# Reordering a hand-scheduled kernel of two state-space layers: 26 moves in the list of operations, five of them with another engine or form

## The chip, the cores and the metric

The kernel runs on one core of one Trainium2 chip. Its time is the device time of that core for one execution, in microseconds (us); of several executions the median is taken. The core has five engines with queues of their own, each in order: TensorE (PE, with its weight loads shown as PEld), VectorE (DVE), ScalarE (ACT), GpSimd (POOL) and SyncE (SP), which issues nearly all DMAs. Matrix products land in PSUM, eight banks of 128 x 512 float32, and are copied from there ("evicted") by DVE or ACT.

## The reference

Two independent layers on sequences of 2048 steps and 640 channels, their results side by side in bf16. Layer A is a diagonal complex recurrence, layer B a gated long convolution.

```python
# A
Lam_bar = exp(dt * Lam); B_bar = ((Lam_bar - 1) / Lam)[:, None] * Bmat
Bu = einsum("bld,pd->blp", x, B_bar)
h[t] = Lam_bar * h[t-1] + Bu[t]
a = 2 * einsum("blp,dp->bld", h, Cmat).real + x * Dskip
# B
k_shift = sum over 4 taps of shift_k * shifted k
kv = k_shift * v
y = irfft(rfft(kv padded) * rfft(ssm_k padded))[:2048] + kv * ssm_D
b = q * y
out = concatenate([a, b], -1)
```

## The kernel before, in words

The program is a list of 815 small operations, built first and then emitted in an order written out by hand. Every operation has a number, the engines that may run it, what it reads and writes, and, where it uses PSUM, a group that holds one or two banks. The string `ORDER` lists all of them: `266V6` means operation 266, on DVE, bank 6. The letters are A (ACT), V (DVE), G (POOL), T (PE) and S (SP); a small `t` is PE in the narrow form, in which a product with 128 columns of weights is issued as two with 64. The order of one engine's entries is that engine's program order. Between engines only data and banks matter: an instruction waits for the operations whose data it needs, and the first of a group for the last of the group that held its bank.

```python
order = [(int(x[:-2]), x[-2].upper(), int(x[-1])) for x in ORDER.split()]
...
if o is o.group.ops[0]:
    need |= {held[b] for b in own if held[b] is not None}
```

Some entries issue nothing. A product with an addition or multiplication after the eviction (`ev_C`, `er1`) does both at once on DVE; on ACT it only copies, and a following `em_C` or `em1` does the rest. Where the first ran on DVE, the second is empty.

Layer A. The 16 steps of a chunk are treated as a tree: `up2`, `up1`, `up0` (lines 581 and 602, evicted at 598, 622, 648) combine pairs of steps by the tables `rr` (line 457; operations 143 to 146, one for each power), the 128 chunk ends go through a coarse scan, and `dn3` to `dn0` (line 225 or 229, added on DVE at 728 or evicted by ACT at 726) go back down. The coarse scan is done twice, for five blocks each: `cs_v` turns the vector on PE, `cs_v_m` (line 679) multiplies it by a sine, `cs_a` (682) by a cosine, `cs_w` (683) takes the difference, `cs_s` (684) is the scan, then `cs_k`, `cs_k_m` (679), `cs_b` (687) and `cs_h` (690) turn back. The operations of the first are 318 to 326, of the second 327 to 335. `gm` (175, line 457) scales C for `gC` (line 571, evicted at 575); six small copies `cf` (137 to 142, lines 206 and 449) feed it. Last, 16 projections `C0` to `C15` (line 225 wide, 229 narrow) add x times D: `ld_r` (line 736) loads the rows of x, `xd` (737) multiplies them by D's row, which `ld_Dr` (operation 91, line 372) has spread over all partitions, `ev_C` (754) adds, `st_A` (765) stores. `ld_C1` (270 and 272, line 556) loads the last block of C, its real and imaginary half.

Layer B. For each of five blocks of channels, k and v are loaded transposed (`ld_k`, `ld_v`, line 814), four taps are multiplied (`cm`, lines 205 on DVE and 206 on ACT) and added (`ca`, 840), multiplied by v (`cx`, 841), stored to a buffer in DRAM (`pl`, 847) and read back in another layout by eight transfers for each half of the channels (`rl`, 857). The taps of all blocks share one buffer, so block d+1's k is loaded when block d's taps are done. The convolution is a two-stage transform on PE: `s1` (lines 876 wide, 881 narrow, evicted at 886), `s2` (900, evicted at 913), a product on DVE or POOL (`pp`, `pq`, `py`, `pz`, lines 924 to 931), and back by `r2` (951, evicted at 956) and `r1` (972, evicted at 988 or 990). It is run for the filter (`h`, loaded at line 807, and its first row added to at 809) and for kv (`k`), in two halves 0 and 1. The filter of half 1 is loaded into the room of the coarse scan's buffers, so its loads wait for `cs_h1`.

The tables of sines start as integer products on POOL (`wqh` line 309, `gqh` line 350, `cph` line 475, with the counters `w_m`, `g_m`) and become sines on ACT (`w_s` 314, `g_s` 354).

Of the kernel before, what the change touches and what calls it, by code (L numbers as in the profile page):

```python
# [1097 lines left out]
def plain_order(P):  # L1098
# [16 lines left out]


ORDER = (
# [40 lines left out]
)  # L1158


# [68 lines left out]
```

## Time and profile before

| | |
|---|---|
| median of 3 runs | 188.11 us |
| lowest, highest | 187.65, 189.12 us |
| the profiled execution | 187.3 us from its first to its last instruction |
| busy: PE, PEld | 175.6, 126.3 us |
| busy: DVE, ACT, POOL | 158.0, 147.7, 72.6 us |
| granted TensorE clock | 0.999 |
| bytes moved by DMA | 30.15 MB |

The profile is of one execution. Its page gives the span from first to last instruction and no time around it, so the span is taken as that execution's own time. Times of rows are microseconds from the start of the span. A row of the timeline has start, length, engine, line, operation, what it writes and reads, how many instructions, and in brackets how long the engine was idle before and who released it. Operations that are given by number are found in such rows by counting along their engine's order.

### The profile page before, as it was taken

How to read it: one execution, taken by the hardware profiler on the slowest of the kernel's cores; microseconds unless marked ns; L12 is line 12 of the kernel's file. 1: busy time of each engine (PE TensorE's matmuls, PEld its weight loads, DVE VectorE, ACT ScalarE, POOL GpSimd, SP SyncE). 2: the span in 40 equal slices, each digit the busy share in tenths (PEclk: the TensorE clock that was granted, in tenths of full speed). 3: DMA queues.
4: the chain of work that ended last, by engine and by line, in shares of the span. 5: the costliest groups of instructions: out<-in, count | busy, mean ns of one | idle time of the engine just before them, and what ended most of it. 6: DMA issues, size and time to landing. Idle time of an engine off the chain costs nothing.

```text
span 187.3 us, 7665 instructions
## 1 busy us (share of the span) xinstructions
PE 175.6 (94%) x3398; PEld 126.3 (67%) x3399; DVE 158.0 (84%) x225; ACT 147.7 (79%) x181; POOL 72.6 (39%) x68
## 2 busy tenths in 40 slices
PE   7998999999799979979997999999999999999992
PEld 2565666677468756656685688776588876887770
DVE  3537964679959899999969999899999999998961
ACT  2469699989899979999997997997898883985000
POOL 8679999900000000008803925730740000551620
PEclk9999999999999999999999999999999999999999
DMA  5999999799999989999989479402496993058996
GB/s 153 191 184 158 200 143 140 141 174 182 198 253 154 290 179 152 180 182 154 138 109 251 154 170 133 75 5 72 122 196 120 210 227 85 15 160 187 208 219 173
DMA packets 106682, 30.15 MB, mean 161 GB/s; under 512 B 101274, under 2 KB 106010, under 8 KB 106650
## 3 DMA queue, kind: packets, MB, share of 16 engines
q1 hardware_dynamic: 106332, 29.35, 86.7%
q8 instruction: 26, 0.43, 1.1%
q10 hardware_dynamic: 318, 0.33, 0.6%
q14 instruction: 6, 0.05, 0.1%
HBM read 11.32 MB, written 7.86 MB: 102 GB/s over the span
## 4 chain that ended last, share of the span: by engine, by line
PE 54%; DVE 23%; DMA 9%; ACT 8%; issue 3%; DVEq 0%; ACTq 0%
PE acc L225 17%; PE acc L581 13%; DMA arena<-in_B_k_dram 9%; PE acc L229 6%; DVE arena L728 6%; PE acc L900 6%; DVE arena L205 5%; ACT arena L913 5%; PE acc L951 4%; DVE arena L840 3%; PE acc L972 3%; PE acc L539 2%; DVE arena L754 2%; PE acc L881 1%; ACT arena L886 1%
## 5 line engine op out<-in xcount | busy, mean ns | idle before, releaser
L581 PE MATMUL acc<-arena 128*64 128x512 bf16 x400 | 45.6, 380 | 1.8 <-DVE arena L457 1.1
L913 ACT CAST arena<-acc 128x960 bf16<-128x960 f32 (+1 forms) x43 | 37.4, 916 | 4.0 <-PE acc L900 2.2
L225 PE MATMUL acc<-arena 128*128 128x320 bf16 (+2 forms) x255 | 36.4, 297 | 2.2 <-DVE arena L754 1.1
L581 PEld LDWEIGHTS <-arena 128*64 128x64 bf16 x400 | 26.0, 110 | 17.8 <-DVE arena L457 1.3
L886 ACT CAST arena<-acc 128x1024 bf16<-128x1024 f32 x37 | 35.8, 1034 | 2.1 <-PE acc L881 2.0
L225 PEld LDWEIGHTS <-arena 128*128 128x128 bf16 x256 | 23.7, 98 | 12.1 <-DVE arena L754 1.3
L841 POOL TENSOR_TENSOR arena<-arena 128x2048 bf16<-128x2048 bf16 x2 | 8.8, 4410 | 53.7 <-DVE arena L840 46.1
L900 PE MATMUL acc<-arena 128*64 128x160 bf16 x512 | 23.6, 235 | 1.8 <-DVE arena L679 1.4
L900 PEld LDWEIGHTS <-arena 128*64 128x64 bf16 x512 | 18.6, 110 | 8.3 <-ACT arena L913 2.2
L229 PE MATMUL acc<-arena 128*64 128x320 bf16 (+3 forms) x258 | 23.2, 313 | 0.5 <-DVE arena L690 0.5
L840 DVE TENSOR_TENSOR arena<-arena 128x2048 bf16<-128x2048 bf16 x14 | 17.6, 1256 | 4.5 <-ACT arena L206 4.3
L728 DVE TENSOR_TENSOR arena<-acc,arena 128x1024 bf16<-128x1024 f32 (+2 forms) x19 | 20.4, 1114 | 0.9 <-PE acc L229 0.5
L760 POOL TENSOR_TENSOR arena<-arena 128x640 bf16<-128x640 f32 x3 | 4.2, 1416 | 32.6 <-ACT arena L752 32.6
L956 ACT CAST arena<-acc 128x1024 bf16<-128x1024 f32 x16 | 15.4, 1025 | 1.7 <-PE acc L951 1.6
L229 PEld LDWEIGHTS <-arena 128*64 128x64 bf16 x258 | 13.0, 110 | 3.5 <-DVE arena L690 0.6
L876 PE MATMUL acc<-arena 128*64 128x128 bf16 x400 | 14.6, 220 | 0.2 <-ACT arena L886 0.2
L876 PEld LDWEIGHTS <-arena 128*64 128x64 bf16 x400 | 12.9, 110 | 2.4 <-ACT arena L886 0.9
L205 DVE TENSOR_SCALAR arena<-arena 128x2048 bf16<-128x2048 bf16 x15 | 11.0, 749 | 3.6 <-DMA arena<-in_B_k_dram 3.5
L754 DVE TENSOR_TENSOR arena<-acc,arena 128x640 bf16<-128x640 f32 x13 | 10.7, 820 | 3.5 <-PE acc L225 2.2
L206 ACT ACTIVATE arena<-arena 128x2048 bf16<-128x2048 bf16 (+2 forms) x10 | 11.1, 1112 | 1.5 <-DMA arena<-in_B_k_dram 1.5
L924 DVE TENSOR_TENSOR arena<-arena 128x2560 bf16<-128x2560 bf16 x8 | 11.9, 1484 | 0.1
L602 PE MATMUL acc<-arena 128*64 128x256 bf16 (+2 forms) x140 | 11.6, 291 | 0.1
(142 smaller groups left out, 284.4 us busy)
## 6 DMA issues: line engine op xcount, KB each, us to landing
out_dram<-arena SPq DMA_DIRECT2D x32, 160.0 KB, 3.3
arena<-in_B_ssm_k_dram SPq DMA_DIRECT2D x8, 320.0 KB, 6.1
kv_rows<-arena SPq DMA_DIRECT2D x5, 512.0 KB, 4.7
arena<-kv_rows SPq DMA_DIRECT2D x16, 160.0 KB, 4.0
arena<-in_A_x_dram SPq DMA_DIRECT2D x16, 160.0 KB, 3.5
arena<-in_B_q_dram SPq DMA_DIRECT2D x8, 320.0 KB, 6.3
arena<-in_A_B_im_dram ACTq DMA_DIRECT2D x1, 160.0 KB, 2.8
arena<-in_A_B_re_dram SPq DMA_DIRECT2D x1, 160.0 KB, 3.0
```

The source lines that it names most:

```text
L205: vm = lambda e: lambda out, in_, by: e.tensor_scalar_mul(out=out, in0=in_, scalar1=by)
L225: e.matmul(out, lhsT=lhsT, rhs=rhs, start=start, stop=stop, skip_group_check=True)
L229: e.matmul(out[half], lhsT=lhsT[:, half], rhs=rhs, start=start, stop=stop, skip_group_check=True, tile_position=(0, 64 * r))
L581: e.matmul(o[64 * r:64 * r + 64], lhsT=self.BT[j][:, r, d, :], rhs=self.XP[:, d, 2 * q:2 * q + 2], start=(d == 0), stop=(d == 4), skip_gro ...
L728: e.tensor_tensor(out=o, in0=b, in1=o, op=ALU.add)
L754: e.tensor_tensor(out=two(ys), in0=two(B)[:, :, 0:320], in1=two(ys), op=ALU.add)
L840: P.add(f"ca{d}_{j}", tt, lambda e: e.tensor_tensor(out=t1, in0=t1, in1=t2, op=ALU.add), outs=[t1], ins=[t1, t2])
L876: e.matmul(B[64 * b:64 * b + 64, 128 * i:128 * i + 128], lhsT=lh[i], rhs=F[:, b, :], start=True, stop=True, tile_position=(0, 64 * b))
L886: P.add(f"e1{what}{hf}_{u}", {PACT: act(1024), PDVE: dve(1024)}, lambda e, B: c.CP[e](out=out, in_=(B.rearrange("p (l n s k) -> p k s l n" ...
L900: e.matmul(B[64 * s:64 * s + 64, 512 * b + 160 * i:512 * b + 160 * i + 160], lhsT=c.W[:, k, 64 * b:64 * b + 64], rhs=self.AS[hf][:, k, 160 ...
L913: c.CP[e](out=out, in_=b.rearrange("p r (k j n) -> p r k j n", k=n, j=4) if nj > 1 else b.rearrange("p r (k x) -> p r k x", k=n))
L956: P.add(f"er2{hf}_{u}", {PACT: act(1024), PDVE: dve(1024)}, lambda e, B: c.CP[e](out=out, in_=B.rearrange("p (s n b) -> p b s n", s=2, n=4 ...
```

## The change

Only `ORDER` changes. Every operation keeps its bank. On each queue the order differs as follows (names and numbers as in the list; "passes" means that it now comes before):

- SP: D's row `ld_Dr` (91) passes `ld_v3` (445), `ld_r0`, `ld_k4` (455), one half of `ld_C1` (270), `ld_r1` and the four `ld_h1` (439 to 442). `rl0_10` (412) passes five transfers and comes right behind `pl2` (410). `ld_C1` (272) falls behind `rl0_21`, `rl0_31`, `ld_Dr`, `ld_v3`, `ld_k4` and 270. `ld_r0` (724) and `ld_r1` (729) fall behind the four `ld_h1`. The two `ld_B2` (173, 174) change places.
- DVE: the coarse scan's links 319, 321 and 322 come before the taps 447 and 446 of block 3; 325 comes among the additions of block 3, 324 before the tap 451. The table products `rr1` (144) and `gm` (175, with the copy 137 before it) come before `cx0` (387) and `cx1` (398). 133 passes one eviction, 134 falls behind 384 and 385. 679 passes 559, and 715 passes 719.
- ACT: `ev_up20_4` (214) and `w_s` (49) fall behind `ev_up1_2` (238); the copies 142 and 139 come before `e1h0_2` (194).
- POOL: four of the table operations (47, 52, 54, 77) come later; 713 passes 706.
- PE: `cs_v0` (318) passes `s2h0_30` (313); `s2h0_27` (311) falls behind 299 and 259, which change places.
- Another engine or form: `cm0_0` (385) ACT to DVE; `ev_up0b_8` (266) DVE to ACT; `xd2` (735) POOL to DVE; `e2k1_27` (666) ACT to DVE; `dn2_5` (344) from the narrow form to the wide one.

The diff, cut to these places:

```diff
-  ... 173S0 ... 174S0 ... 155S0
+  ... 174S0 173S0 ... 155S0
...
-  ... 380A0 ... 214A2 ... 218A0 ... 49A0 ... 385A0 ... 53A0 ... 75A0 ... 238A0
+  ... 380A0 ... 218A0 ... 384V0 385V0 134V0 ... 53A0 ... 75A0 ... 238A0 214A2 ... 49A0
...
-  ... 387V0 ... 396V0 144V0 ... 135V0 145V0 ... 397V0 ... 398V0 ... 403V0 194A2 137V0 ... 142A0 ... 139A0 ... 175V0
+  ... 144V0 387V0 ... 396V0 ... 135V0 145V0 ... 397V0 ... 138A0 ... 142A0 137V0 139A0 175V0 398V0 ... 194A2 ... 403V0
...
-  320V0 316V0 ... 447V0 301T4 ... 313T0 446V0 ... 318t2 ... 319V2 ... 448V0 ... 321V0 ... 449V0 ... 322V0 ... 450V0 ... 451V0
+  320V0 318t2 319V2 321V0 316V0 322V0 ... 313T0 ... 447V0 ... 446V0 ... 325V0 448V0 ... 449V0 ... 450V0 ... 324V4 451V0
...
-  ... 410S0 415S0 158S0 414S0 416S0 413S0 412S0 272S0 417S0 418S0 445S0 724S0 455S0 270S0 729S0 440S0 441S0 442S0 439S0 91S0 734S0
+  ... 410S0 412S0 415S0 158S0 414S0 416S0 413S0 417S0 418S0 91S0 445S0 455S0 270S0 272S0 440S0 441S0 442S0 439S0 724S0 729S0 734S0
...
-  309T4 ... 311T2 ... 259T6 299T0 ... 266V6 ... 344t4 ... 735G0 ... 666A6
+  309T4 ... 299T0 259T6 311T2 ... 266A6 ... 344T4 ... 735V0 ... 666V6
```

(Each line shows the entries of the queues concerned in their order; "..." are entries left out.)

78 rows, old and new, of the table ORDER are left out of this document.

## The prediction

> **What bounds the kernel now.** I read the page first, then the stretches, then the idle time before each matmul and each VectorE (DVE) operation in order of time.
>
> ```profile
> span 187.3 us, 7665 instructions
> PE 175.6 (94%) x3398; PEld 126.3 (67%) x3399; DVE 158.0 (84%) x225; ACT 147.7 (79%) x181; POOL 72.6 (39%) x68
> ```
>
> ```profile
> 65.20:97.80 32.60, 29.37 (x695) 21.06 (x696) 30.98 (x39) 31.08 (x40) 8.14 (x2) 1.00 1.05 159
> 99.40:183.60 84.20, 83.22 (x1928) 63.74 (x1928) 78.20 (x87) 61.04 (x70) 30.42 (x15) 1.00 0.69 147
> ```
>
> The columns are stretch, length, then busy time of PE, PEld, DVE, ACT and POOL, granted clock (1.00 throughout), DMA share. Two regimes: from 65 to 98 DVE (30.98 of 32.60) and ScalarE (ACT, 31.08) are full while PE idles 3.2 us; from 99.4 on PE is full (83.22 of 84.20). So work saved before 99.4 counts only if the first matmul after 99.37 starts earlier, and what is added after it counts only if PE is made to wait. The three longest waits of PE after 20 us:
>
> ```profile
> 48.12 2.13 PE L581 MATMUL acc<-arena 128*64 128x512 bf16 x18 [1.15 <-DVE arena L457]
> ...
> 67.41 0.61 PE L900 MATMUL acc<-arena 128*64 128x160 bf16 x12 [1.39 <-DVE arena L679]
> ...
> 99.37 2.89 PE L225 MATMUL acc<-arena 128*128 128x320 bf16 x20 [0.97 <-DVE arena L754]
> ```
>
> They are up0a_2 (239) waiting for the table rr1 (144), s2h0_27 (311) waiting for the bank that cs_v0_m (319) drains, and C1 (731) waiting for ev_C0 (727). Together 3.51 us; the change touches the cause of all three.
>
> **The change part by part.** *The table product 144.*
>
> ```profile
> 37.89 1.23 DVE L841 TENSOR_TENSOR arena<-arena 128x2048 bf16<-128x2048 bf16 x1 [1.83 <-DMA arena<-in_B_v_dram]
> ...
> 46.58 1.48 DVE L457 TENSOR_TENSOR arena<-arena 128x1280 bf16<-128x1280 bf16 x1
> ```
>
> It goes from 46.58 to ahead of cx0 (387), where DVE idles 1.83 for the landing of v: 1.48 fits. PE then starts up0a_2 at 46.97 (the end of the matmuls before it), 1.15 earlier. Next late is ACT, which evicts for PE there:
>
> ```profile
> 51.79 1.01 ACT L886 CAST arena<-acc 128x1024 bf16<-128x1024 f32 x1 [0.85 <-PE acc L881]
> 52.82 0.21 ACT L206 ACTIVATE arena<-arena 64x5 bf16<-64x5 f32 x1
> ...
> 58.80 0.22 ACT L206 ACTIVATE arena<-arena 64x5 bf16<-64x5 f32 x1
> ```
>
> The copies 142 and 139 (0.21, 0.22) move into that 0.85 of idle, so e1h0_2 starts near 51.3, not 51.79, and everything behind loses another 0.43: about 0.5 + 0.4 = 0.9 at 60. PE waits for ACT's ev_up0a_4 before up0b_4 (58.67 now), so of the 1.15 some 0.9 arrive at cs_v0.
>
> POOL runs until 37.89 beside the new place:
>
> ```profile
> 35.64 1.25 POOL L475 TENSOR_TENSOR arena<-arena 128x640 int32<-128x640 int32 x1
> 36.85 1.03 POOL L350 TENSOR_TENSOR arena<-arena 128x512 int32<-128x512 int32 x1
> ```
>
> ```profile
> 18.66 3.74 DVE L457 TENSOR_TENSOR arena<-arena 128x1280 bf16<-128x1280 bf16 x2
> ```
>
> Two such products beside POOL took 3.74, so the one that was stretched 2.3 (3.74 less 1.48, and the overlap of 0.08 back). At 2.3, 144 ends at 38.4, cx0 0.5 later, and e1h0_6 (202) behind it at 40.8; up1_0 needs its bank at 41.08: still nothing. The Trainium skill, "SBUF — State Buffer", § SBUF: two separate sides, says that a VectorE operation with two SBUF inputs and a GpSimd one that reads SBUF exclude each other, and the later one blocks fully. The rows show a stretch at most; the sum by it is rival D.
>
> *The product gm (175) and the coarse scan.*
>
> ```profile
> 64.40 0.44 PE L229 MATMUL acc<-arena 128*64 128x512 bf16 x4
> ```
>
> ```profile
> 62.64 1.48 DVE L457 TENSOR_TENSOR arena<-arena 128x1280 bf16<-128x1280 bf16 x1
> 64.05 0.48 DVE L682 TENSOR_TENSOR arena<-arena 128x640 bf16<-128x640 bf16 x1
> ...
> 65.20 1.42 DVE L205 TENSOR_SCALAR arena<-arena 128x2048 bf16<-128x2048 bf16 x2 [0.65 <-DMA arena<-in_B_k_dram]
> 66.53 0.82 DVE L679 TENSOR_TENSOR arena<-acc,arena 128x640 bf16<-128x640 f32 x1
> ...
> 72.10 0.75 DVE L205 TENSOR_SCALAR arena<-arena 128x2048 bf16<-128x2048 bf16 x1
> 72.77 0.82 DVE L679 TENSOR_TENSOR arena<-acc,arena 128x640 bf16<-128x640 f32 x1
> 73.60 0.45 DVE L648 CAST arena<-acc 128x256 bf16<-128x256 f32 x1
> 73.94 0.48 DVE L687 TENSOR_TENSOR arena<-arena 128x640 bf16<-128x640 bf16 x1
> ...
> 78.24 1.49 DVE L684 TENSOR_TENSOR_SCAN arena<-arena 128x640 bf16<-128x640 f32 x1
> ```
>
> gm goes to about 51.3 to 52.8, behind the copies that feed it, ahead of cx1 (398), which becomes about 2 us later; behind cx1 stands the next idle for k2, and its only reader, the store pl1, issues at 58.30: covered. Without gm, cs_a0 (320) starts at 62.65. Now 319 follows at once and waits for PE: cs_v0 ran to 64.84; it is 0.9 earlier and passes s2h0_30 (313), some 0.2 more, so 319 starts at about 63.75 where DVE is free from 63.1: a new wait of 0.65 in place of the old 0.65 for k3. From 62.64 to the end of the second scan (79.73) the sum is: gm 1.41 out (64.05 − 62.64), ev_up0b_8 (266, to ACT) 0.34 out (73.94 − 73.60), the idle 0.65 out, the wait 0.65 in, and 0.35 in for three more pairs in which an operation needs the one just before it (such a pair starts 0.03 after the end, others 0.08 before it). Net −1.4. PE's 1.39 at 67.41 goes, but its next banks wait for ACT, and cs_k1 waits for the second scan: PE, too, gets 1.4. ACT keeps up: it idled 1.0 before ev_up0c_6 here, more than the 0.45 that 266 adds. Conv 3 (447, 446) starts at 66.5, 1.3 later, and ends its taps near 72.9 as before, so ld_k4 is not held up. All of DVE, ACT and PE is then 1.4 earlier up to 95.
>
> *D's row and the transfers.*
>
> ```profile
> 67.63 3.23 SPq L857 DMA_DIRECT2D arena<-kv_rows  x4
> 70.90 1.79 SPq L556 DMA_TRANSPOSE arena<-in_A_C_im_dram  x1
> ...
> 82.93 7.61 SPq L807 DMA_DIRECT2D arena<-in_B_ssm_k_dram  x4
> 90.58 3.45 SPq L372 DMA_DIRECT2D arena<-in_A_Dskip_dram  x1
> ```
>
> ```profile
> 95.96 0.53 DVE L809 TENSOR_TENSOR arena<-arena 128x80 bf16<-128x80 bf16 x1
> 97.87 0.49 DVE L737 TENSOR_TENSOR arena<-arena 128x640 bf16<-128x640 bf16 x1 [1.38 <-DMA arena<-in_A_Dskip_dram]
> ```
>
> ld_Dr (91) leaves its place behind the four loads of h1 and goes ahead of v3, near 72. But xd0 (725) multiplies ld_r0 (724) by D, and 724 and 729, which had been issued at 77.68 and 81.83, move to that very place behind h1. Dr took 3.45 to issue and landed 7.3 after its issue began, because the queue was full of h1. ld_r0 has the same 160 KB and stands in the same queue, so I give it Dr's time: the 1.38 of DVE and the 0.97 of PE stay, with another name on them. From both sides: it may land up to 1.4 sooner (DVE asks for it at 95.1) or 0.5 later. h1 itself is issued when cs_h1 (335) ends (82.78 now, 1.4 earlier then), so landing and C1 move by 1.4. v3 and k4 get 160 KB ahead of them, but rl0_10 (412) now fills SP's wait for the landing of pl2 (67.63), and ld_C1 (272, 1.79) leaves; both halves of C1 land near 83, gC4_0 needs them at 85.6: covered by 2 us. v4, behind three row loads now instead of Dr and one, keeps about 1 of the 1.4; its relay has over 3 us before s1k1 at 121. Swapping 173 and 174 changes nothing: up20_4 needs both.
>
> *The five operations in another form or engine.*
>
> ```profile
> 32.33 1.45 DVE L840 TENSOR_TENSOR arena<-arena 128x2048 bf16<-128x2048 bf16 x1 [2.52 <-ACT arena L206]
> ```
>
> ```profile
> L205 DVE TENSOR_SCALAR arena<-arena 128x2048 bf16<-128x2048 bf16 x15 | 11.0, 749 | 3.6 <-DMA arena<-in_B_k_dram 3.5
> ```
>
> cm0_0 (385) on DVE costs 0.75 where DVE idled 2.52 before ca0_0, waiting for ACT's form of it; ACT's 2.0 are taken up by w_s (49) and ev_up20_4 (214), moved behind, and PE is full from 18.6 to 47: 0. If that cover were gone, the 2.0 would be the gain; PE shows no wait for it.
>
> ```profile
> 138.96 2.91 PE L229 MATMUL acc<-arena 128*64 128x320 bf16 x40
> ```
>
> dn2_5 (344) in the wide form: C7, narrow, took 2.91 here and C1, wide, 2.89 above; 0, between −0.1 and 0.1 of its 0.76. xd2 (735) from POOL to DVE:
>
> ```profile
> 112.53 0.82 DVE L754 TENSOR_TENSOR arena<-acc,arena 128x640 bf16<-128x640 f32 x1 [0.37 <-PE acc L229]
> ```
>
> 0.49 (the row of xd0) against 0.37 of idle, less one overlap of 0.08: 0.04 at most. e2k1_27 (666) from ACT to DVE is the one that costs:
>
> ```profile
> 132.18 6.09 DVE L728 TENSOR_TENSOR arena<-acc,arena 128x1024 bf16<-128x1024 f32 x5
> 138.18 1.48 DVE L924 TENSOR_TENSOR arena<-arena 128x2560 bf16<-128x2560 bf16 x1
> ```
>
> ```profile
> L913 DVE CAST arena<-acc 128x960 bf16<-128x960 f32 x3 | 3.5, 1154 | 0.0
> ```
>
> ```profile
> 135.91 1.24 DVE arena L728
> ...
> 137.19 1.93 PE acc L900 x48
> ```
>
> It enters between the second and third of five additions (365, then 377, 361, 371) that run 132.18 to 138.27 without a gap over 0.08 and release PE's banks; in the chain that ended last, 361 (135.91) hands on to s2k1_16 (137.19). 1.15 more, less three overlaps of 0.08 and the two gaps of 0.08 that close, puts 361 0.76 later; s2k1_16 and, behind it in the same bank, C7 follow. PE has no slack there, and what ACT saves nobody waits for. Cost 0.76, bounds 0.4 (an input ready sooner) and 1.15.
>
> The POOL moves keep the same products done by 38, and the moves of 679, 713 and 715 pass only entries that issue nothing.
>
> **Sum:** −1.4 at C1, +0.76 at 137: −0.6 of 187.3, 186.7. The nearest timed run stands 0.3 above the span, the median 188.11 stands 0.8 above: **187.5**.
>
> **The rivals.** *A, nothing waits at xd0.* ld_r0 has 1,280-byte rows of its own, Dr reads one row 128 times; if that, not the queue, made Dr slow, DVE and PE save up to another 1.4 and 0.97 at 98: 1.4 + 0.97 − 0.76 gives 1.6 saved, 186.5; with 666 at its lower bound 186.1. Against: r2, issued right behind Dr, had an ordinary source and was not quick either. Chance 0.25.
>
> *B, slower: the early gain stops at ACT.* If ACT does not catch up from 51 to 60, cs_v0 ends at 64.6, DVE waits 1.5 before 319, and the 1.4 shrinks to 0.5; with ld_r0 landing 0.5 later than Dr in its place nothing is left at C1, and 666 remains: +0.76, 188.9. It decides from a gain at C1 under 0.76. For it: ACT is full from 52 to 61. Chance 0.2.
>
> *C, DVE sets the end.* DVE's busy time rises by 0.75 + 0.49 + 1.15 − 0.45 = 1.94; were DVE the bound throughout, the time would be 190.1. The rows against it: 385 and 735 fall into idle of 2.52 and 0.37. The Trainium skill, "Perfetto Trace Analysis", § Identifying the Most-Contended Engine, judges TensorE not by matmul occupancy but by LDWEIGHTS (67% here) and would so put DVE's 84% first. The trace agrees up to 98 (DVE 30.98 of 32.60) and not behind 99.4, where PE's 83.22 of 84.20 leave less room than DVE's 78.20. Chance 0.08.
>
> *D, 144 is kept out by POOL.* If it starts only behind POOL's last product (37.9), e1h0_6 ends at 41.8, up1_0 and all PE work up to up0a_2 come 0.7 later, 0.45 of the 1.15 is left, cs_v0 comes 0.45 later than forecast, and so does C1: 187.9. Against: the stretch above was 0.85 at most. Chance 0.07.
>
> **How the numbers follow.** Forecast 0.37 (187.0 to 188.0 by itself), A 0.25, B 0.2, C 0.08, D 0.07, other 0.03. The range takes in A, B and D with their bounds: 185.9 to 189.4. This kernel's three runs lie 0.8% apart, so under 1% (186.2 to 190.0) is no change that can be told. Faster by more needs all of A, with 666 at its lower bound or a larger gain at the scan: 0.2; slower by more is C, the rest and the far end of B: 0.13; same 0.67.
>
> **What would show it.** Right: no wait before up0a_2 near 47; 319 ahead of conv 3 with a wait for PE; xd0 still waiting, now for A_x; C1 near 98.0; the addition before s2k1_16 (361) held up, and s2k1_16 near 136.6. Wrong: xd0 without a wait (A), a C1 not earlier than 98.6 (B), or 361 following 377 with idle before it (666 free).

## The result, and the profile after

| | median of all runs | ratio to the kernel before, 95% interval | span of the profile |
|---|---|---|---|
| kernel before, 18 runs | 187.77 us | 1 | 187.3 (first profile) |
| changed kernel, 18 runs | 189.56 us | 1.0077 (1.0057 to 1.0097) | 188.9 |
| changed kernel, second set, 6 runs | 189.68 us | 1.0163 (1.0118 to 1.0207) | 189.0 |
| changed kernel, third set, 6 runs | 189.60 us | 1.0141 (1.0104 to 1.0179) | 187.7 |

Each ratio is taken over the executions without those more than 1.5% above the fastest of their kernel, so it is not the quotient of the two medians (1.0095 in the first set).

The forecast was 187.5, a gain of 0.6. By the ratios the change makes the kernel slower, by 1.4 us in the first set and by 3.0 and 2.6 us in the second and third. Its own median is nearly the same in all three. The kernel before stood at 187.77 in the first set and between 186.69 and 187.00 in the five later ones, which ran on five different chips; why the first set differs is open. The profiled execution of the changed kernel took 190.64 with a span of 188.9, so about 1.7 us lie around the span.

The profile of the changed kernel follows: first the head of its page, then rows of DVE, PE and SP.

```profile
span 188.9 us, 7654 instructions
PE 176.3 (93%) x3395; PEld 125.1 (66%) x3395; DVE 164.3 (87%) x227; ACT 146.0 (77%) x180; POOL 72.7 (39%) x67
```

```profile
36.71 2.54 DVE L457 TENSOR_TENSOR arena<-arena 128x1280 bf16<-128x1280 bf16 x1
39.17 2.05 DVE L841 TENSOR_TENSOR arena<-arena 128x2048 bf16<-128x2048 bf16 x1
41.15 1.21 DVE L886 CAST arena<-acc 128x1024 bf16<-128x1024 f32 x1
...
52.67 1.49 DVE L457 TENSOR_TENSOR arena<-arena 128x1280 bf16<-128x1280 bf16 x1 [2.08 <-ACT arena L206]
54.08 1.22 DVE L841 TENSOR_TENSOR arena<-arena 128x2048 bf16<-128x2048 bf16 x1
55.21 0.75 DVE L205 TENSOR_SCALAR arena<-arena 128x2048 bf16<-128x2048 bf16 x1
...
64.84 0.82 DVE L679 TENSOR_TENSOR arena<-acc,arena 128x640 bf16<-128x640 f32 x1 [0.53 <-PE acc L229]
...
81.50 0.90 DVE L690 TENSOR_TENSOR arena<-arena 128x640 bf16<-128x640 bf16 x1
...
97.59 0.52 DVE L809 TENSOR_TENSOR arena<-arena 128x80 bf16<-128x80 bf16 x1 [1.89 <-DMA arena<-in_B_ssm_k_dram]
98.32 0.49 DVE L737 TENSOR_TENSOR arena<-arena 128x640 bf16<-128x640 bf16 x1 [0.21 <-DMA arena<-in_A_x_dram]
```

```profile
42.41 2.35 PE L581 MATMUL acc<-arena 128*64 128x512 bf16 x20 [0.64 <-DVE arena L886]
...
48.08 2.33 PE L581 MATMUL acc<-arena 128*64 128x512 bf16 x20
...
98.21 1.00 PE L881 MATMUL acc<-arena 64*64 64x64 bf16 x96 [1.05 <-DVE arena L809]
99.83 1.40 PE L225 MATMUL acc<-arena 128*128 128x320 bf16 x9 [0.62 <-DVE arena L754]
...
136.14 0.62 PE L229 MATMUL acc<-arena 128*64 128x512 bf16 x4 [0.46 <-DVE arena L913]
...
138.41 1.78 PE L900 MATMUL acc<-arena 128*64 128x160 bf16 x46 [0.23 <-DVE arena L728]
```

```profile
67.69 5.32 SPq L857 DMA_DIRECT2D arena<-kv_rows  x5
...
81.95 2.21 SPq L556 DMA_TRANSPOSE arena<-in_A_C_im_dram  x1
84.32 8.77 SPq L807 DMA_DIRECT2D arena<-in_B_ssm_k_dram  x4
```

The waits that the change was to remove are gone: PE has none before up0a_2 (48.08) and none before s2h0_27 for the bank that cs_v0_m drains. Others stand in their place. 144 (36.71) takes 2.54 and cx0 2.05, so the eviction 202 ends at 42.36 and up1_0 waits 0.64 for its bank. gm (52.67) waits 2.08 for ACT's copies, and cx1 and conv 2 (55.21, 53.96 in the first profile of the kernel before) stand behind it. ld_C1 (81.95) holds SP, so h1 starts at 84.32, 1.9 after cs_h1 has ended (81.50 + 0.90). The addition to the first row of h1 (line 809, called addD1 below) waits 1.89 for it, and PE waits 1.05 for addD1 (98.21). 666 holds up 360, whose bank it empties, by 0.46, and s2k1_16 by 0.23. C1 is at 99.83 (99.37 before), s2k1_16 at 138.41 (137.19 before).

### The profile page after: what moved, and what is told of

The parts are those of the page before. It is cut to its first block, busy times and chain, and to the rows that moved or that the text cites. A ratio compares the mean times of both kernels' runs of the same rounds, so it can differ in the third digit from the quotient of the medians.

```text
span 188.9 us, 7654 instructions
## 1 busy us (share of the span) xinstructions
PE 176.3 (93%) x3395; PEld 125.1 (66%) x3395; DVE 164.3 (87%) x227; ACT 146.0 (77%) x180; POOL 72.7 (39%) x67
## 4 chain that ended last, share of the span: by engine, by line
PE 46%; ACT 16%; DVE 13%; SPq 10%; DMA 9%; issue 3%; DVEq 0%; ACTq 0%
PE acc L225 17%; PE acc L581 10%; ACT arena L886 5%; PE acc L951 5%; ACT arena L913 5%; SPq L807 4%; PE acc L900 4%; DVE arena L728 4%; SPq L547 4%; DMA arena<-in_A_B_re_dram 4%; PE acc L229 4%; DMA arena<-in_A_x_dram 3%; PE acc L972 3%; DMA arena<-in_B_k_dram 3%; PE acc L602 2%
## 5 line engine op out<-in xcount | busy, mean ns | idle before, releaser
L225 PE MATMUL acc<-arena 128*128 128x320 bf16 (+3 forms) x260 | 37.2, 297 | 1.5 <-DVE arena L754 0.6
L581 PEld LDWEIGHTS <-arena 128*64 128x64 bf16 x400 | 25.5, 110 | 18.5 <-DVE arena L435 1.5
L841 POOL TENSOR_TENSOR arena<-arena 128x2048 bf16<-128x2048 bf16 x2 | 8.1, 4072 | 54.2 <-DVE arena L840 43.5
L229 PE MATMUL acc<-arena 128*64 128x320 bf16 (+3 forms) x250 | 22.7, 314 | 1.0 <-DVE arena L913 0.5
L900 PEld LDWEIGHTS <-arena 128*64 128x64 bf16 x512 | 18.7, 110 | 7.1 <-ACT arena L913 1.8
L840 DVE TENSOR_TENSOR arena<-arena 128x2048 bf16<-128x2048 bf16 x14 | 17.1, 1222 | 1.9 <-ACT arena L206 1.7
L229 PEld LDWEIGHTS <-arena 128*64 128x64 bf16 x250 | 12.5, 110 | 3.9 <-DVE arena L913 0.6
L876 PEld LDWEIGHTS <-arena 128*64 128x64 bf16 x400 | 12.6, 110 | 2.7 <-ACT arena L886 1.0
L205 DVE TENSOR_SCALAR arena<-arena 128x2048 bf16<-128x2048 bf16 x16 | 12.3, 786 | 0.3
L309 POOL TENSOR_TENSOR arena<-arena 128x512 int32<-128x512 int32 x8 | 11.9, 1502 | 0.1
L457 DVE TENSOR_TENSOR arena<-arena 128x1280 bf16<-128x1280 bf16 x5 | 10.0, 2021 | 2.1 <-ACT arena L206 2.1
```

Source lines behind the costliest of these rows:

```text
L205: vm = lambda e: lambda out, in_, by: e.tensor_scalar_mul(out=out, in0=in_, scalar1=by)
L225: e.matmul(out, lhsT=lhsT, rhs=rhs, start=start, stop=stop, skip_group_check=True)
L229: e.matmul(out[half], lhsT=lhsT[:, half], rhs=rhs, start=start, stop=stop, skip_group_check=True, tile_position=(0, 64 * r))
L309: P.add("wqh", {G: 1.0}, lambda e, mx=mx, qx=qx: e.tensor_tensor(out=qx.rearrange("p (k b c) -> p k b c", k=4, b=2), in0=bc(mx.rearrange(" ...
L581: e.matmul(o[64 * r:64 * r + 64], lhsT=self.BT[j][:, r, d, :], rhs=self.XP[:, d, 2 * q:2 * q + 2], start=(d == 0), stop=(d == 4), skip_gro ...
L840: P.add(f"ca{d}_{j}", tt, lambda e: e.tensor_tensor(out=t1, in0=t1, in1=t2, op=ALU.add), outs=[t1], ins=[t1, t2])
```

## Was the first profile of the kernel before like the others?

**A second profile of it** (no edit).

> The kernel before itself, a second profile of it. Theory (its first profile was one of its longest executions, and its waits for transfers are larger than usual): span near 185, no wait of DVE for k1 (0.90 in the first) and none for k3 (0.65), the wait of PE before s2h0_27 (311) 0.2 or less instead of 1.39, a smaller wait for D's row than 1.38. Rival (the three long waits that the forecast set out from are the rule): they stand there again within 0.3.

Measured: 186.30 us, span 184.5 (so 1.8 lie around the span, and the execution profiled first, with its span of 187.3, was the one of 189.12). Its timeline on DVE and on PE, and the first three rows behind PE's start in its table of what PE waited for (line, cause, us in all, times, longest):

```profile
35.79 2.05 DVE L841 TENSOR_TENSOR arena<-arena 128x2048 bf16<-128x2048 bf16 x1
37.76 1.21 DVE L886 CAST arena<-acc 128x1024 bf16<-128x1024 f32 x1
38.89 1.40 DVE L205 TENSOR_SCALAR arena<-arena 128x2048 bf16<-128x2048 bf16 x2
...
44.31 1.48 DVE L457 TENSOR_TENSOR arena<-arena 128x1280 bf16<-128x1280 bf16 x1
...
52.09 0.76 DVE L205 TENSOR_SCALAR arena<-arena 128x2048 bf16<-128x2048 bf16 x1 [2.30 <-DMA arena<-in_B_k_dram]
...
62.65 1.42 DVE L205 TENSOR_SCALAR arena<-arena 128x2048 bf16<-128x2048 bf16 x2
...
95.15 0.49 DVE L737 TENSOR_TENSOR arena<-arena 128x640 bf16<-128x640 bf16 x1 [0.77 <-DMA arena<-in_A_Dskip_dram]
```

```profile
46.53 2.35 PE L581 MATMUL acc<-arena 128*64 128x512 bf16 x20
...
96.66 2.89 PE L225 MATMUL acc<-arena 128*128 128x320 bf16 x20 [0.43 <-DVE arena L754]
```

```profile
PE acc L225 <- ACT arena L886: 0.8, 1, 0.8
PE acc L225 <- DVE arena L754: 0.6, 2, 0.4
PE acc L229 <- DVE arena L690: 0.5, 1, 0.5
```

Here v, k1 and k3 are in time: DVE does not wait before cx0 (1.83 in the first profile), nor before conv 1 (0.90) or conv 3 (0.65). 144 runs at 44.31 and is done at 45.79, before PE wants it at 46.53. Of the 3.51 us of PE's waits from which the forecast set out, 0.43 are left. C1 stands at 96.66, 2.7 earlier than in the first profile.

The profiles of the kernels below bear this out. Nine of the later profiles, this one with them, have 144 in its old place, and none has a wait before up0a_2; seven have gm and the scan in their old places, and none has one before s2h0_27. Only the wait at C1 comes back, at 0.38 to 0.51 us in the six of these profiles in which D's row stands in its old place. The theory holds: the two longest waits belonged to one long execution, and what made it long is open.

One row matters for what follows: cx0 takes 2.05 here, where it stands beside POOL's last products, and took 1.23 in the first profile, where it began when POOL had ended (37.89).

## The parts, each alone on the kernel before

**144 ahead of cx0.**

```diff
- 188V0 387V0 202V4 ... 396V0 144V0
+ 188V0 144V0 387V0 202V4 ... 396V0
```

> The kernel before with one move: the table product 144 ahead of cx0 (387). Theory 3 (POOL and DVE keep each other out there): 144 takes 2.3 to 2.6, cx0 behind it ends 0.7 to 1.5 later, up1_0 waits 0.3 to 0.6 for 202, up0a_2 no longer waits; from cx1 on DVE stands as in the kernel before, within 0.3; the time within 0.2% of the kernel before. Rival (PE's early work sets the coarse scan): 0.3 to 0.5% quicker.

Measured: 1.0042 (1.0015 to 1.0069), 0.8 us slower. DVE, POOL and PE of this kernel:

```profile
36.02 2.54 DVE L457 TENSOR_TENSOR arena<-arena 128x1280 bf16<-128x1280 bf16 x1
38.48 2.06 DVE L841 TENSOR_TENSOR arena<-arena 128x2048 bf16<-128x2048 bf16 x1
```

```profile
35.96 1.25 POOL L475 TENSOR_TENSOR arena<-arena 128x640 int32<-128x640 int32 x1
37.17 2.29 POOL L350 TENSOR_TENSOR arena<-arena 128x512 int32<-128x512 int32 x1
```

```profile
41.73 2.35 PE L581 MATMUL acc<-arena 128*64 128x512 bf16 x20 [0.71 <-DVE arena L886]
```

The rows read as turns: POOL's first product ends at 37.21; 144, begun at 36.02, ends 1.35 behind it (38.56); POOL's next one, which takes 1.03 alone, ends 0.90 behind that (39.46); cx0 ends 1.08 behind that (40.54). Alone they take 1.48, 1.03 and 1.23, so to within 0.15 us nothing runs side by side. cx0 is no slower than in the second profile above (2.05); it ends 2.7 later, which is about the length of 144 and not the 0.7 to 1.5 expected. The mechanism was as expected, the time was not, and neither was the rival's: no wait was there to be removed, so PE's new 0.71 stays to C1 (97.53, 0.87 later than in the second profile).

**gm ahead of cx1, with its copies.**

```diff
- (DVE) 397V0 398V0 403V0 137V0 ... 409V0 175V0    (ACT) 138A0 194A2 142A0 ... 139A0
+ (DVE) 397V0 137V0 175V0 398V0 403V0 ... 409V0    (ACT) 138A0 142A0 139A0 194A2
```

> The kernel before with gm (175) and its copies (137 on DVE, 142 and 139 on ACT) ahead of cx1 and of e1h0_2, as in the change, and nothing else. Theory 4 (gm ahead of cx1 waits for ACT, and conv 2, k3 and SP's chain behind them come later): gm waits 1.0 to 2.1 for ACT, conv 2 starts 0.7 to 1.3 later, conv 3's first tap waits for k3 again, h1 starts later by 0.5 to 1; 0.3 to 0.7% above the kernel before. Rival (the 1.41 that gm no longer takes behind cx2 is the larger): 0.2 to 0.4% quicker.

Measured: 1.0063 (1.0033 to 1.0093), 1.2 us slower. DVE and PE:

```profile
51.23 1.49 DVE L457 TENSOR_TENSOR arena<-arena 128x1280 bf16<-128x1280 bf16 x1 [2.56 <-ACT arena L206]
...
53.77 0.75 DVE L205 TENSOR_SCALAR arena<-arena 128x2048 bf16<-128x2048 bf16 x1
...
63.66 1.42 DVE L205 TENSOR_SCALAR arena<-arena 128x2048 bf16<-128x2048 bf16 x2 [0.76 <-DMA arena<-in_B_k_dram]
```

```profile
65.86 0.61 PE L900 MATMUL acc<-arena 128*64 128x160 bf16 x12 [1.04 <-DVE arena L679]
```

Conv 2 starts 1.7 later than in the second profile of before (53.77 against 52.09); so do its taps' end and the load of k3, and conv 3 and PE wait (0.76, 1.04). That is theory 4, with larger waits than it expected: gm's is 2.56, not 1.0 to 2.1.

**666 on DVE.**

```diff
- ... 365V4 ... 666A6 377V0
+ ... 365V4 666V6 377V0
```

> The kernel before with one change: e2k1_27 (666) on DVE instead of ACT, between 365 and 377. Theory 1 (it holds up 361 and s2k1_16): 0.7 slower, 0.3 to 0.4% above the kernel before. Rival (the kernel with 666 back on ACT was no quicker than the changed one, so 666 costs nothing that stays to the end): within 0.15%.

Measured: 1.0045 (1.0015 to 1.0075), 0.84 us. PE waits as in the changed kernel:

```profile
132.86 0.62 PE L229 MATMUL acc<-arena 128*64 128x512 bf16 x4 [0.46 <-DVE arena L913]
...
135.12 1.85 PE L900 MATMUL acc<-arena 128*64 128x160 bf16 x48 [0.23 <-DVE arena L728]
```

**The scan's links.**

```diff
- (DVE) 320V0 316V0 447V0 446V0 319V2 448V0 321V0 449V0 322V0 ...    (PE) 313T0 318t2 ... 311T2 259T6 299T0    266V6
+ (DVE) 320V0 319V2 321V0 316V0 322V0 447V0 446V0 325V0 448V0 ...    (PE) 318t2 313T0 ... 299T0 259T6 311T2    266A6
```

> The kernel before with the scan's links alone: 319, 321, 322, 325 and 324 ahead of conv 3's taps as in the change, cs_v0 ahead of s2h0_30, 299 and 259 ahead of 311, ev_up0b_8 on ACT; gm stays behind cx2. Theory (the forecast's gain stood on waits that only the first profile shows): a new wait of 0.5 to 0.9 before 319, the 0.45 of ev_up0b_8 saved, cs_h1 within 0.4 of the second profile of the kernel before, time within 0.2%. Rival (the forecast: the links spare DVE its waits): cs_h1 0.6 to 1.4 earlier, time 0.3 to 0.7% below.

Measured: 1.0004 (0.9980 to 1.0028), as the theory has it. The wait before 319 is there, and cs_h1 ends at 80.86 (80.45 in the second profile of the kernel before):

```profile
63.30 0.83 DVE L679 TENSOR_TENSOR arena<-acc,arena 128x640 bf16<-128x640 f32 x1 [0.88 <-PE acc L229]
```

**SP's queue, whole and in two halves.**

```diff
- 173S0 174S0 ... 410S0 415S0 158S0 414S0 416S0 413S0 412S0 272S0 417S0 418S0 445S0 724S0 455S0 270S0 729S0 440S0 441S0 442S0 439S0 91S0
+ 174S0 173S0 ... 410S0 412S0 415S0 158S0 414S0 416S0 413S0 417S0 418S0 91S0 445S0 455S0 270S0 272S0 440S0 441S0 442S0 439S0 724S0 729S0
```

> The kernel before with SP's queue in the changed order, the other engines as before. Theory 2 (ld_C1 and D's row keep SP from h1): ld_h1 starts 1.0 to 1.8 after the end of cs_h1 instead of 0.15, addD1 waits 0.8 to 1.9 for h1, and xd0 0.2 or more for the row of x; C1 0.2 to 0.9 later than in the second profile of the kernel before, time 0.1 to 0.4% above. Rival (the wait for D's row, 0.77 in that profile, is gone, and h1 had room): C1 0.4 earlier, time 0.2% below.

> The kernel before with the two ld_B2 (173, 174) in the changed order and nothing else. Theory 5 (the swap makes the half that PE waits for later: over the profiles so far up20_4 stands near 18.9 with it, near 18.4 without): up20_4 at 18.7 to 19.2, 0.1 to 0.35% above the kernel before, and the executions of two lengths. Rival (both halves are needed anyhow, and the start scatters by itself): within 0.1%.

> The kernel before with SP's queue in the changed order, but the two ld_B2 as before. Theory 2 (h1 late): h1 0.8 or more behind cs_h1, addD1 waits 0.5 to 1.5 for it, C1 0.1 to 0.6 later than in the second profile of the kernel before, time 0 to 0.3% above. Rival (D's row gains more than h1 loses): 0.1 to 0.3% below.

Measured: whole 1.0005 (0.9966 to 1.0043), the swap of 173 and 174 alone 1.0007 (0.9985 to 1.0029), the rest alone 0.9992 (0.9971 to 1.0013). The whole had executions of two lengths, most near 186.2 or 188.5, and the profiled one was of the longer kind (h1 0.9 behind cs_h1, 1.24 of waiting before addD1); the halves did not, and what makes the two lengths is open. SP and DVE of the rest alone:

```profile
65.12 5.32 SPq L857 DMA_DIRECT2D arena<-kv_rows  x5
...
78.79 1.27 SPq L556 DMA_TRANSPOSE arena<-in_A_C_im_dram  x1
80.98 7.32 SPq L807 DMA_DIRECT2D arena<-in_B_ssm_k_dram  x4
```

```profile
94.45 0.63 DVE L737 TENSOR_TENSOR arena<-arena 128x640 bf16<-128x640 bf16 x1
95.64 0.82 DVE L754 TENSOR_TENSOR arena<-acc,arena 128x640 bf16<-128x640 f32 x1 [0.56 <-PE acc L229]
```

SP is done with ld_C1 at 80.06 here, before cs_h1 ends (80.85), and xd0 waits for no transfer. The order alone thus need not make h1 late, and theory 2 falls as far as the time goes. In the changed kernel the same queue is done at 84.16, 4.1 later, where cs_h1 ends 1.55 later: it starts 2.6 later (67.69 against 65.12), behind gm and conv 2, and its issues take 1.5 longer, for a reason that is open. Theory 5 falls too: with the swap alone up20_4 started at 18.52, 18.40 in the second profile of the kernel before. In the three profiles of the changed kernel it starts at 19.09 to 19.39; why is open, and the kernel without 144, gm and 666 (next section), which has the swap, loses nothing.

## The changed kernel, with parts taken out

**Without 144, gm and 666** (each back in its old place and engine).

```diff
- ... 144V0 387V0 ... 137V0 175V0 398V0 ... 142A0 139A0 194A2 ... 666V6 377V0
+ ... 387V0 ... 396V0 144V0 ... 398V0 403V0 137V0 ... 409V0 175V0 ... 194A2 142A0 ... 139A0 ... 666A6
```

> The changed kernel with three parts back in their old places: 144 behind cm1_0, gm with its copies behind cx2 (and 142, 139 on ACT), 666 on ACT. Theory (these three are the whole cost): within 0.3% of the kernel before. Rival (the other moves cost too, such as 385, 133 and 134 among POOL's products, or SP's order): 0.4% or more above.

Measured: 1.0000 (0.9979 to 1.0022). Everything else in the change, 385, 735, 344, SP's order and the scan's links with it, comes to nothing to within 0.2%, and without the three the loss is gone. Each alone costs 0.42, 0.63 and 0.45%, in sum 1.50%, where the changed kernel itself stood 1.63 and 1.41% above in its two later sets.

**gm behind cx1.**

```diff
- 137V0 175V0 398V0 403V0
+ 137V0 398V0 175V0 403V0
```

> The changed kernel with gm (175) behind cx1 (398) instead of ahead of it. Theory 4 (ahead of cx1, gm held up cx1 and conv 2 for ACT's copies): the idle of about 2.1 before gm shrinks to about 0.9, conv 2 (403) starts about 1.1 earlier, and as long as PE and ACT keep up, so do cx2, the coarse scan and h1; the end 0.3 to 1.0 earlier than the changed kernel. Rival (cs_v0 on PE, not DVE, sets the scan): DVE waits for PE before 319 by 1.6 instead of 0.53, and the end stays within 0.3.

Measured: 1.0063 (1.0038 to 1.0089), where the changed kernel of the same set had 1.0163: 1.75 us of it gone by one exchange. Both waits came as the theory and its rival had them, on DVE:

```profile
52.12 1.49 DVE L457 TENSOR_TENSOR arena<-arena 128x1280 bf16<-128x1280 bf16 x1 [0.88 <-ACT arena L206]
53.53 0.75 DVE L205 TENSOR_SCALAR arena<-arena 128x2048 bf16<-128x2048 bf16 x1
...
64.29 0.82 DVE L679 TENSOR_TENSOR arena<-acc,arena 128x640 bf16<-128x640 f32 x1 [1.41 <-PE acc L229]
```

That is more than the 1.1 by which conv 2 was to come earlier. SP's queue may explain the rest, which no run shows by itself: it issues without a gap over 0.3 from the landing of pl2 to h1, so it starts earlier with conv 2, and h1 starts 0.3 behind cs_h1 (82.15 in this profile) instead of 1.9:

```profile
82.15 7.72 SPq L807 DMA_DIRECT2D arena<-in_B_ssm_k_dram  x4
```

**Three more, and the changed kernel twice.** 666 back on ACT; SP's queue as before; 144 behind 202, where POOL has ended:

```diff
- 666V6 377V0            - 410S0 412S0 415S0 ...      - 144V0 387V0 202V4 391V0
+ 377V0 ... 666A6        + 410S0 415S0 158S0 ...      + 387V0 202V4 144V0 391V0
```

> The changed kernel with e2k1_27 (666) back on ACT, nothing else. Theory 1 (666 on DVE holds up the addition 361, s2k1_16 and all PE work behind it): 361 again directly behind 377 and 365, s2k1_16 0.7 us nearer to the front (its delay against the kernel before falls from 1.2 to about 0.5), end 0.7 earlier: about 0.4% above the kernel before instead of 0.8%. Rival (the delay of 0.5 that stands at 135 already is what sets the end; DVE behind 137 has no slack for itself either): the end moves by 0.2 or less.

> The changed kernel with SP's whole queue in the order of the kernel before (D's row, the two rows of x, rl0_10, half of C1, the two ld_B2), the other engines as changed. Theory 2 (SP's queue makes h1 late): the first ld_h1 starts when cs_h1 has ended (82.4) instead of 84.3, the 1.9 of waiting before addD1 goes, xd0 waits for D's row again, C1 starts about 0.4 earlier than in the kernel before and 0.85 earlier than in the changed one; end 0.8 to 0.9 earlier, so about 0.3% above the kernel before. up20_4 near 19 us loses its 0.44. Rival (C1 is set by DVE's work, not by the transfers): C1 stays within 0.2 of the changed kernel's.

> The changed kernel with the table product 144 moved from ahead of cx0 to behind the eviction 202, where POOL has ended its products. Theory 3 (POOL and DVE kept each other out: 144 took 2.54 and cx0 2.05): 144 takes 1.48, 202 ends near 40 instead of 42.36, up1_0 has no wait of 0.64 and starts 0.9 or more earlier, up0a_2 still has no wait; the matmuls of the convolution from 48 to 60 come 0.9 to 1.3 earlier. At C1 nothing of it is left, since DVE's conv 2 and the transfers set it: end within 0.3 of the changed kernel. Rival (the products are slow for another reason, such as DMA traffic into SBUF): 144 takes over 2 us at its new place too, and up0a_2 waits for it. Rival (PE's early work sets the end after all): end 0.9 earlier.

> The changed kernel itself, a second profile of it beside the others of this set. Theory (the first profile, 190.64, was one of its longer executions, and the profile of the kernel before, 189.12, one of that kernel's longest): 0.6 to 0.9% above the kernel before; the profiled span is 0.5 to 2 shorter than 188.9; the same stretches as in the first: 144 over 2.4, cx0 about 2.0, gm behind an idle of about 2.1. Rival (those are accidents of the one profile): 144 near 1.5 and cx0 near 1.2.

> The changed kernel once more, beside the two others. Theory (144, gm and 666 add up, and nothing gains): 1.2 to 1.7% above the kernel before. Rival (part of the three costs lies in the same place, or SP's order gains): 0.6 to 1.1%.

Measured: 1.0094 (1.0065 to 1.0123), 1.0110 (1.0079 to 1.0141) and 1.0060 (1.0030 to 1.0089). The changed kernel was not in that set, so what each took away can only be set against its 1.41 and 1.63% of the later ones: about 0.5 to 0.7 for 666, 0.8 to 1.0 for 144 (0.7 to 0.9 by its median of all runs, 188.38 against 187.00), 0.3 to 0.5 for SP's queue, where the intervals overlap. (666 back on ACT missed its expected 0.4%, which was set against 0.77.) Together with gm's 1.0% from its own set, the parts taken out one at a time come to more than the whole loss. As far as these values go the parts are not independent, and that the costs of the three alone add up to the loss may be chance.

With SP's old order h1 still started 1.05 behind cs_h1 (82.98 against 81.93), and xd0 waited 1.31 for D's row: theory 2 had expected h1 in time. 144 behind 202 took its 1.47 with POOL at rest, and up1_0 did not wait:

```profile
39.18 1.47 DVE L457 TENSOR_TENSOR arena<-arena 128x1280 bf16<-128x1280 bf16 x1
```

The rival, slow through DMA traffic, is out: cx0 took 1.23 in the first profile of the kernel before, with POOL at rest and 284 GB/s of DMA beside it, and 144 took 2.54 beside POOL and 219 GB/s. The theory's other half, an end within 0.3 us of the changed kernel's, does not fit these ratios.

The changed kernel's second set missed the expected 0.6 to 0.9% (1.63), the third met its 1.2 to 1.7. The second profile (an execution of 190.73) has the 2.08 before gm again, 144 at 2.27 and cx0 at 1.21, without a wait of up1_0; the third has 2.08, 2.54 and 2.06, and 0.57 before up1_0. What gm waits for and the stretch of 144 are thus no accident of one profile.

## Three attempts at a better kernel

Three more kernels were run: the kernel before with D's row behind ld_D and nothing else, the changed kernel mended in four places, and the mended one with conv 3's taps ahead of 319.

```diff
- 158S0 414S0 ... 439S0 91S0     - 144V0 387V0 202V4 ... 137V0 175V0 398V0 ... 666V6     - 320V0 319V2 ... 322V0 447V0 446V0
+ 158S0 91S0 414S0 ... 439S0     + 387V0 202V4 144V0 ... 137V0 398V0 175V0 ... 666A6     + 320V0 447V0 446V0 319V2 ... 322V0
```

> The kernel before with one move: D's row (91) is issued behind ld_D (158), where SP stood 1.3 waiting for the landing of pl2; the two rows of x stay where they were. Theory 2 (only the queue behind h1 made D's row late): xd0 has no wait for a transfer, C1 starts 0.97 earlier, ld_h1 starts within 0.5 of 82.9, end 0.6 to 1.0 earlier than the kernel before (0.3 to 0.5%). Rival (addD1 then waits for h1, which starts later by what D's row adds to the queue): a wait of 0.5 to 1.4 before addD1, C1 as before, no difference.

> The changed kernel mended at the four places: 144 behind the eviction 202, gm behind cx1, 666 on ACT, SP's queue as in the kernel before but D's row behind ld_D (158). The scan's links, 385, 735 and 344 stay as changed. Theories 2, 3 and 4 together: no wait of PE before up0a_2 and none at xd0, cs_s0 done about 1.5 earlier than in the kernel before with D's row moved, C1 0.5 to 1.3 earlier than there; time 0.5 to 0.9% below the kernel before, the shortest of all. Rival (SP's queue, full from 66 to 81, sets when h1 starts): ld_h1 no earlier than 80.5, addD1 waits for it, and the time is that of the kernel before with D's row moved (0.2% below).

> The mended kernel (144 behind 202, gm behind cx1, 666 on ACT, SP's queue of the kernel before with D's row behind ld_D) with conv 3's first two taps (447, 446) ahead of cs_v0_m (319) again, where DVE waited 1.41 for PE. Theory (that wait is where the gain of the mended kernel went): the wait before 319 is under 0.1, the second scan ends 0.6 to 0.9 earlier, C1 0.5 or more earlier; time 0.3 to 0.6% below the kernel before. Rival (PE is full from 81 on, and the last stores, issued one behind the other by SP, set the end): C1 within 0.3 and the time within 0.15% of the kernel before.

Measured: 0.9980 (0.9958 to 1.0002), 1.0009 (0.9977 to 1.0041) and 0.9991 (0.9963 to 1.0019): none is told from the kernel before. With D's row early xd0 waits for nothing and addD1 0.35 for h1, but only 0.43 of PE's time hung on D's row. In the mended kernel 319 waits 1.41 for PE, cs_h1 ends at 80.67 (80.45 in the second profile of the kernel before), and h1 starts at 80.86. Its rival had the time and the start of h1 right; the wait of addD1 that it named is not there. With the taps ahead, the wait is for k3 instead (1.47).

## Why the prediction was wrong, step by step

The forecast had a gain of 1.4 us before C1 and a cost of 0.76 behind it. The cost came. The gain did not, and 144 and gm, which the sum had at nothing and at a gain, cost 0.8 and 1.2 us alone.

**What bounds the kernel** is the step that failed first. The sum was made against one profile, whose waits (1.15, 1.39, 0.97) were read as the kernel's; in the second profile they are 0, 0 and 0.43. The step from span to time hid it: the text put the profiled execution 0.3 below the nearest run, and it was that of 189.12, the longest of the three. The gain at C1 leaned on them: on the 0.65 of idle before conv 3, on the 0.9 by which cs_v0 was to come earlier without the 1.15, and on the end of the 1.39. C1 came 0.46 later than in the first profile and 3.2 later than in the second.

**144, "still nothing":** the stretch was sized nearly right (2.3, measured 2.54). What the sum left out is POOL's side of it. It left POOL's next product where it stood (36.85, 1.03); held up by 144, that product ran until 39.46, and cx0, taken at 1.23, took 2.06 beside it. The idle of 1.83 that was to hold 144 is not there when v is in time, and cx0 takes 2.05 without the move too; so 202 comes later by 144's whole stretched length. The part costs 0.42% alone. Rival D, at a chance of 0.07, had the mechanism. The rule of the Trainium skill that was weighed there, "SBUF — State Buffer", § SBUF: two separate sides, says that such an operation takes the port for the whole instruction and the other side blocks. The turns in the rows above agree with it to 0.15 us. The text let "a stretch at most" stand against it; the stretch was the blocking.

**gm, "covered":** the idle behind cx1 was real (2.30 for k2), but gm could not use it from ahead of cx1. It started at 52.67, not 51.3, waiting for copies that ACT makes behind PE's evictions, and it delayed conv 2, k3 and SP's queue. It costs 0.63% alone, where the forecast had a gain of 1.41 us for taking it out from behind cx2.

**The scan, net −1.4:** the 0.65 of idle and the 1.39 of PE were not there to be removed, and the new wait (forecast 0.65) is 0.53 to 1.41 in the profiles. Alone the links give 1.0004.

**D's row:** the text was right in kind that ld_r0 takes D's row's place (xd0 waits 0.21 for the row of x) and wrong that h1 starts with cs_h1. The order alone is neutral.

**666, +0.76:** the size was right. PE's delay against the first profile of the kernel before rose by 0.73 from 132 to s2k1_16, and the part alone cost 0.84. The path was so in part: 0.46 of PE's wait came already at 360, for the bank that 666 empties, which the text did not name, and 0.23 at s2k1_16.

**385, 735, 344 and the swap at nothing:** this was right as a sum with the rest (1.0000). 385 itself took 1.35 beside POOL, not 0.75 (31.29 in the first profile of the changed kernel), without a cost that these runs show.

**The rivals:** C (190.1) and B (188.9) come nearest in the number, but neither in the way it named. Against C, that DVE sets the end: the kernel without 144, gm and 666 keeps DVE busy for 162.7 us, 3.7 more than the second profile of the kernel before, and takes no longer. Against B: in the changed kernel 319 waits 0.53, not 1.5, and the loss hangs on 144, gm and 666.

## What to carry over

A wait for a transfer, and every wait that follows from it, may belong to one execution: look at a second profile before pricing its removal, and check which of the timed runs the profiled one was. An operation put into an idle stretch must have its inputs when the stretch begins and come behind the work that is ready; gm delayed cx1 when it stood ahead of it, with inputs that were not ready. Where two engines take turns, as DVE and POOL do in the rows above, an operation moved beside the other's work costs its own time there and the other's as well (1.48 became 2.54).

## What was not expected of the hardware

VectorE operations of 20 elements a partition also wait for POOL's turn. Below is the same one (132, whose place on DVE is as before, while POOL's order beside it has changed), each time with what POOL ran beside it, in the first profile of the kernel before and then in that of the changed one:

```profile
26.30 0.17 DVE L437 TENSOR_TENSOR arena<-arena 128x20 f32<-128x20 f32 x1
```

```profile
26.28 0.57 POOL L305 IOTA arena<- 128x512 int32 x1
```

```profile
26.57 1.02 DVE L437 TENSOR_TENSOR arena<-arena 128x20 f32<-128x20 f32 x1
```

```profile
25.84 1.71 POOL L350 TENSOR_TENSOR arena<-arena 128x512 int32<-128x512 int32 x1
```

132 took 0.17 beside a counter of POOL, whose row reads nothing, and 1.02 beside a product, ending 0.04 behind it (27.59 and 27.55). 133 and 134 went the same way (0.37 and 0.16 to 0.97 and 1.01). DVE's busy time rose by 6.3 us in all, 158.0 to 164.3, where the forecast had 1.94; the kernel without 144, gm and 666, which still has 133 at 0.99 and 134 at 1.01, took no longer than the kernel before, so the stretches of 133 and 134 lie in time that DVE had to spare.
